# SwiGLU FFN on one core: gate and up of tokens 1024 to 2047 as seven block products instead of eight

## The chip, the cores and the metric

The kernel runs on one NeuronCore of a Trainium2 chip. A core has five engines with a queue each: TensorE (matmuls; PE in the profile), VectorE (DVE), ScalarE (ACT), GpSimd (POOL) and SyncE (SP, which here only issues DMAs). Matmuls write to PSUM, eight banks of 128 partitions by 512 fp32 numbers; VectorE and ScalarE read PSUM, and everything else lies in SBUF. The metric is the device time of the launch in microseconds.

## The reference

`x` has 2048 tokens of 512 numbers, `w_gate` and `w_up` are 512 by 1376, `w_down` is 1376 by 512, all in bf16:

```python
g = _silu(x @ w_gate)
u = x @ w_up
return (g * u) @ w_down
```

## The kernel before

Tokens are cut into four chunks c of 512 (`SC`), the 1376 hidden columns into ten tiles ft of 128 and a rest of 96, the 512 inputs into four blocks dk of 128. x lies transposed in `xT_sb` (block, token); the first 256 tokens are transposed on TensorE (the T groups), the others by transposing DMAs (`load_x`, one for tokens 256 to 511 and one per later chunk). SyncE issues all loads in one order (`loads_on_sync`): the first x, the weights in five slabs (gate, up), the last 32 up columns, x1, x2, x3, then `w_down`.

For each chunk and tile, a gate group and an up group of matmuls run on TensorE (`gu_step`, line 346): for each dk two half-wide matmuls of 64 weight columns each, 512 tokens, side by side in the array, into one PSUM bank. ScalarE writes silu of the gate bank to `sg_sb` (fp32, line 294), VectorE multiplies it with the up bank into `hT_sb` in bf16 (line 308). The rest of 96 columns is done by one X group per chunk (line 408) and one Y group per two chunks (line 419): their products go into `ht_sb`, in which each chunk has a strip of 32 partitions, and `hl_sb`.

Then comes the down stage. A product of an output tile of 128 tokens is summed over ten 128-row tiles of hidden columns and the rest. `strips` (line 455) cuts the 128 rows into four strips of 32 and runs four output tiles (a quad: one of each chunk) side by side, each in another strip of the array, in four turns; `whole_rows` (line 432) does the last quad with full 128-row matmuls. The finished bank is copied to `o_sb` by VectorE (line 312) or ScalarE and stored by a DMA.

The order on each engine is written out by hand as one list per engine: TensorE goes through chunk 0, 1, 2, 3 (tiles 0 to 9, then X), then Y, then down. A list of groups gives each group the next of the eight banks in turn, and a group waits until the readers of the group eight before it are done (`free`). Semaphores count finished groups (`s_P`) and finished operations of ScalarE and VectorE (`s_A`, `s_D`). GpSimd only makes one index pattern at the start (`iota`, line 278).

```python
for m in (0, HC):
    ins = pe.matmul(
        g["bank"][m:m + HC, n0:n1], lhsT=w_sb[:, dk, col + m:col + m + HC],
        rhs=xT_sb[:, dk, c * SC + n0:c * SC + n1], start=(dk == 0), stop=(dk == KD - 1),
```

Of the kernel before, what the change touches and what calls it, by code (L numbers as in the profile page):

```python
# [7 lines left out]
FP32 = mybir.dt.float32  # L8

N_WARM = 6  # L10
N_FILL = 1


def bass_standalone__swiglu_ffn__prompt_kernel(nc, x, w_gate, w_up, w_down, out):
# [3 lines left out]
    KD = D // P  # L18
    NFF = F // P
    NFT = NFF + 1  # L20
# [13 lines left out]
    NSG = 4  # L34
    NOS = 8
    assert D == 512 and S % SC == 0 and KD == 4 and F_LAST == 96 and NSC % 2 == 0
# [4 lines left out]

    UPH = F + 32
    WTOT = 2 * F
    XC0 = NFF * P
    YC0 = UPH + NFF * P

    with ExitStack() as es:
# [5 lines left out]
        w_sb = sb("w_sb", [P, KD, WTOT], BF16)  # L53
# [7 lines left out]
        sg_sb = [sb(f"sg_sb{i}", [P, SC], FP32) for i in range(NSG)]  # L61
        sgx_sb = [sb(f"sgx_sb{c}", [P, SC], FP32) for c in range(NSC)]
        sgy_sb = [sb(f"sgy_sb{c}", [P, SC], FP32) for c in range(NSC)]
        yu_sb = [sb(f"yu_sb{i}", [P, SC], FP32) for i in range(NSC // 2)]
        o_sb = [sb(f"o_sb{i}", [P, D], BF16) for i in range(NOS)]
        psum = ps("psum", [P, NB, 512], FP32)
        banks = [psum[:, i, :] for i in range(NB)]
        turn = [0, 2, 1, 3, 4, 5, 6, 7]

# [4 lines left out]
        s_I = sem("s_I")  # L74
        s_J = sem("s_J")
        s_P = sem("s_P")
        s_A = sem("s_A")
        s_D = sem("s_D")
        s_T = sem("s_T")
        s_dma = [sem(f"s_dma{i}") for i in range(4 * NOS)]  # L80
        rest = list(range(4 * NOS))

        def take(i):
            rest.remove(i)
            return s_dma[i]
# [3 lines left out]
        loads = {}  # L89

        def load_sem(name):
            loads[name] = take(homes[name] if name in homes else rest[0])
            return loads[name]
# [4 lines left out]


        def load_x(eng, name, t0, t1):  # L100
            eng.dma_start_transpose(
                xT_sb[:, :, t0:t1], xf[t0:t1, :]
            ).then_inc(load_sem(name), 16)

        def load_w(eng, name, src, base, f0, f1):
            eng.dma_start(
                w_sb[:, :, base + f0:base + f1],
                src[:, f0:f1].rearrange("(k p) f -> p k f", p=P),
            ).then_inc(load_sem(name), 16)

        slabs = [(0, 2), (2, 4), (4, 6), (6, 8), (8, NFT)]
        slab_of = {ft: a for a, b in slabs for ft in range(a, b)}

        def load_slab(eng, a, b):
            load_w(eng, f"wg{a}", w_gate, 0, a * P, min(b * P, F))
            load_w(eng, f"wu{a}", w_up, UPH, a * P, min(b * P, F - 32))

        def loads_on_sync(sp):
            sp.dma_start(
                xn_sb[:, :, :].rearrange("p j d -> p (j d)"), xf[0:HT, :].rearrange("(p j) d -> p (j d)", j=NXN)  # L120
            ).then_inc(load_sem("xn"), 16)
            load_slab(sp, *slabs[0])
            load_x(sp, "x0b", HT, SC)
            for a, b in slabs[1:]:
                load_slab(sp, a, b)
            load_w(sp, "wut", w_up, F - (F - 32), F - 32, F)
            for c in range(1, NSC):
                load_x(sp, f"x{c}", c * SC, (c + 1) * SC)
            sp.dma_start(
                wd_sb[:, 0:NFF, :], w_down[0:NFF * P, :].rearrange("(k p) d -> p k d", p=P)  # L130
            ).then_inc(load_sem("wd"), 16)
            for c in range(NSC):
                sp.dma_start(
                    wdt_sb[R * c:R * (c + 1), :, :], w_down[NFF * P:F, :].rearrange("(q p) d -> p q d", p=R)
                ).then_inc(load_sem(f"wdt{c}"), 16)
            sp.dma_start(wdl_sb[:, :], w_down[NFF * P:F, LASTA:D]).then_inc(load_sem("wdl"), 16)

        groups = []  # L140
        n_read = {"A": 0, "D": 0}
        act_ops, dve_ops = [], []

        def add_group(kind, **what):
            g = dict(kind=kind, at=len(groups), bank=banks[turn[(len(groups) - KD) % NB]], readers=[], **what)
            groups.append(g)
            return g

        def add_op(eng, g, **what):
            n_read[eng] += 1  # L150
            op = dict(g=g, at=n_read[eng], **what)
            (act_ops if eng == "A" else dve_ops).append(op)
            if g:
                g["readers"].append((eng, op["at"]))
            return op
# [7 lines left out]
        sg_reader = []  # L163
        n_sg = 0
        h_ready = {}

        def plan_tiles(c, fts):
            nonlocal n_sg
            gates = [add_group("G", c=c, ft=ft) for ft in fts]
            ups = [add_group("U", c=c, ft=ft) for ft in fts]  # L170
            for ft, gg, gu in zip(fts, gates, ups):
                b = n_sg % NSG
                free = sg_reader[n_sg - NSG] if n_sg >= NSG else 0
                a = add_op("A", gg, kind="silu", out=sg_sb[b][:, :], src=gg["bank"][:, :], free=free)
                d = add_op(
                    "D", gu, kind="mul", out=hT_sb[:, ft, c * SC:(c + 1) * SC], a=sg_sb[b][:, :],
                    b=gu["bank"][:, :], after=a["at"],
                )
                sg_reader.append(d["at"])
                h_ready[c] = d["at"]  # L180
                n_sg += 1
# [4 lines left out]
        LC = NSC - 1  # L186
        t_ready = {}

        def plan_x(c):
            g = add_group("X", c=c)  # L190
            y0, y1 = yblk(c)
            add_op("A", g, kind="silu", out=sgx_sb[c][96:128, :], src=g["bank"][64:96, :], free=0)
            a = add_op("A", g, kind="silu", out=sgy_sb[c][y0:y1, :], src=g["bank"][0:64, :], free=0)
            add_op(
                "D", g, kind="mul", out=ht_sb[R * c:R * (c + 1), 2, :],
                a=sgx_sb[c][96:128, :], b=g["bank"][96:128, :], after=a["at"] - 1,
            )
            if c == LC:
                add_op(
                    "D", g, kind="mul", out=hl_sb[2 * R:3 * R, :],  # L200
                    a=sgx_sb[c][96:128, SC - P:SC], b=g["bank"][96:128, SC - P:SC], after=a["at"] - 1,
                )

        def plan_y(pi):
            g = add_group("Y", pi=pi)
            a = add_op("A", g, kind="copy", out=yu_sb[pi][:, :], src=g["bank"][:, :], stored=(None, 0))
            for c in (2 * pi, 2 * pi + 1):
                y0, y1 = yblk(c)
                if c == LC:
                    add_op(  # L210
                        "D", None, kind="mul", out=hl_sb[0:2 * R, :],
                        a=sgy_sb[c][y0:y1, SC - P:SC], b=yu_sb[pi][y0:y1, SC - P:SC], after=a["at"],
                    )
                for q in range(2):
                    r0, r1 = y0 + R * q, y0 + R * (q + 1)
                    d = add_op(
                        "D", None, kind="mul", out=ht_sb[R * c:R * (c + 1), q, :],
# [97 lines left out]
        def on_tensor(pe):  # L315
# [111 lines left out]
            def whole_rows(g, start, stop):  # L427
                if start:
                    free(g)
# [115 lines left out]
```

## Time and profile before

| what | us |
|---|---|
| median of 3 runs | 120.28 (120.11 to 120.47) |
| span of the profiled execution, first to last instruction | 119.3 |
| TensorE busy | 116.5 (98%) |
| VectorE busy | 43.5 (36%) |
| ScalarE busy | 35.5 (30%) |
| GpSimd busy | 0.4 |
| matmuls of gate and up (line 346) | 71.0 summed |

The profile gives no time of the profiled execution beside its span; what lies around the span is seen as the difference to the runs' median. The page lists busy time per engine, the chain of work that ended last (followed back from the last instruction), and groups of instructions with their count, their summed busy time and the mean of one in ns. "Idle before" is how long the engine stood idle before the instructions of a group, and the arrow names what ended that. In the time line a row has start, length, engine, line, what is written and read, and how many instructions were merged into it; the length of a merged row runs from the first start to the last end. A matmul's own duration there includes its way through the array, so that successive matmuls overlap; their spacing is read from the chain, or from the instructions that wait for them.

### The profile page before, as it was taken

How to read it: one execution, taken by the hardware profiler on the slowest of the kernel's cores; microseconds unless marked ns; L12 is line 12 of the kernel's file. 1: busy time of each engine (PE TensorE's matmuls, PEld its weight loads, DVE VectorE, ACT ScalarE, POOL GpSimd, SP SyncE). 2: the span in 40 equal slices, each digit the busy share in tenths (PEclk: the TensorE clock that was granted, in tenths of full speed). 3: DMA queues.
4: the chain of work that ended last, by engine and by line, in shares of the span. 5: the costliest groups of instructions: out<-in, count | busy, mean ns of one | idle time of the engine just before them, and what ended most of it. 6: DMA issues, size and time to landing. Idle time of an engine off the chain costs nothing.

```text
span 119.3 us, 2971 instructions
## 1 busy us (share of the span) xinstructions
PE 116.5 (98%) x1333; PEld 65.9 (55%) x1334; DVE 43.5 (36%) x68; ACT 35.5 (30%) x61; POOL 0.4 (0%) x5
## 2 busy tenths in 40 slices
PE   7999999999999999999999999999999999999993
PEld 2796555555555555555555555554444444464452
DVE  0113534442534452444352444369800040224331
ACT  4225243264242365232454323470000030213001
POOL 1000000000000000000000000000000000000000
DMA  2999999990000000000000000000000023050612
GB/s 97 232 322 347 180 239 246 273 286 17 0 5 0 0 0 0 5 0 5 0 5 0 0 0 0 5 0 0 5 0 0 5 86 96 0 176 17 208 44 88
DMA packets 17564, 8.92 MB, mean 75 GB/s; under 512 B 8592, under 2 KB 17424, under 8 KB 17552
## 3 DMA queue, kind: packets, MB, share of 16 engines
q1 hardware_dynamic: 17408, 8.65, 28.5%
q8 instruction: 10, 0.16, 0.6%
q10 hardware_dynamic: 144, 0.10, 0.3%
q14 instruction: 2, 0.02, 0.1%
HBM read 4.81 MB, written 2.10 MB: 58 GB/s over the span
## 4 chain that ended last, share of the span: by engine, by line
PE 98%; DVE 0%; issue 0%
PE psum L346 59%; PE psum L455 24%; PE psum L432 7%; PE psum L408 3%; PE psum L360 2%; PE psum L419 1%; PE psum L375 0%; PE psum L383 0%; DVE o_sb L312 0%; PE psum L365 0%; PE psum L507 0%
## 5 line engine op out<-in xcount | busy, mean ns | idle before, releaser
L346 PE MATMUL psum<-xT_sb,w_sb 128*64 128x512 bf16 (+1 forms) x672 | 71.0, 374 | 0.0
L346 PEld LDWEIGHTS psum<-xT_sb,w_sb 128*64 128x64 bf16 x672 | 42.7, 112 | 27.4
L308 DVE TENSOR_TENSOR hT_sb<-sg_sb,psum 128x512 bf16<-128x512 f32 x40 | 27.5, 688 | 41.5 <-PE psum L346 36.6
L294 ACT ACTIVATE sg_sb<-psum 128x512 f32<-128x512 f32 x40 | 23.8, 596 | 41.6 <-PE psum L346 41.6
L455 PE MATMUL psum<-wd_sb,hT_sb 32*128 32x512 bf16 x480 | 26.9, 374 | 0.0
L455 PEld LDWEIGHTS psum<-wd_sb,hT_sb 32*128 32x128 bf16 x480 | 12.9, 93 | 13.1 <-issue 0.4
L312 DVE CAST o_sb<-psum 128x512 bf16<-128x512 f32 (+1 forms) x11 | 6.4, 604 | 25.1 <-PE psum L455 19.9
L294 ACT ACTIVATE o_sb<-psum 128x512 bf16<-128x512 f32 (+1 forms) x7 | 3.7, 580 | 33.0 <-PE psum L455 25.9
L432 PE MATMUL psum<-wd_sb,hT_sb 128*128 128x512 bf16 (+2 forms) x59 | 8.7, 307 | 0.2 <-issue 0.2
L432 PEld LDWEIGHTS psum<-wd_sb,hT_sb 128*128 128x128 bf16 x60 | 4.6, 98 | 4.6 <-issue 0.4
L308 DVE TENSOR_TENSOR ht_sb<-sgy_sb,yu_sb 32x512 bf16<-32x512 f32 x8 | 5.5, 683 | 0.4
L408 PE MATMUL psum<-xT_sb,w_sb 128*64 128x512 bf16 x32 | 4.2, 379 | 0.0
L308 DVE TENSOR_TENSOR ht_sb<-sgx_sb,psum 32x512 bf16<-32x512 f32 x4 | 2.8, 691 | 3.5 <-ACT sgx_sb L294 3.5
L294 ACT ACTIVATE sgx_sb<-psum 32x512 f32<-32x512 f32 x4 | 2.4, 588 | 4.5 <-PE psum L408 4.5
L360 PE MATMUL psum<-const-bfloat16-1.0 128*128 128x512 bf16 x6 | 2.7, 623 | 0.8 <-PEq L530 0.8
L455 PE MATMUL psum<-wdt_sb,ht_sb 32*128 32x512 bf16 (+1 forms) x48 | 3.3, 371 | 0.0
L408 PEld LDWEIGHTS psum<-xT_sb,w_sb 128*64 128x64 bf16 x32 | 2.0, 110 | 1.4
L294 ACT ACTIVATE sgy_sb<-psum 64x512 f32<-64x512 f32 x4 | 2.4, 591 | 0.1
L455 PEld LDWEIGHTS psum<-wdt_sb,ht_sb 32*128 32x128 bf16 x48 | 1.3, 93 | 1.3
L419 PE MATMUL psum<-xT_sb,w_sb 128*64 128x512 bf16 x16 | 1.9, 379 | 0.0
L360 PEld LDWEIGHTS psum<-const-bfloat16-1.0 128*128 128x128 bf16 x6 | 0.7, 133 | 1.9 <-issue 1.9
L283 ACT ACT_TABLE_LOAD x1 | 1.3, 1283 | 0.7 <-PEq L530 0.7
(21 smaller groups left out, 7.5 us busy)
## 6 DMA issues: line engine op xcount, KB each, us to landing
out_dram<-o_sb SPq DMA_DIRECT2D x15, 128.0 KB, 1.8
wd_sb<-in_w_down_dram SPq DMA_DIRECT2D x1, 1280.0 KB, 7.8
w_sb<-in_w_gate_dram SPq DMA_DIRECT2D x4, 256.0 KB, 4.0
w_sb<-in_w_up_dram SPq DMA_DIRECT2D x4, 256.0 KB, 4.2
wdt_sb<-in_w_down_dram SPq DMA_DIRECT2D x4, 96.0 KB, 8.1
w_sb<-in_w_gate_dram SPq DMA_DIRECT2D x1, 352.0 KB, 6.3
w_sb<-in_w_up_dram SPq DMA_DIRECT2D x1, 320.0 KB, 6.5
xn_sb<-in_x_dram SPq DMA_DIRECT2D x1, 256.0 KB, 2.8
```

Of the source, the lines that this page charges most:

```text
L283: act.activation(adummy[:, 0:4], zero_c, ACT.Silu)
L294: act.activation(op["out"], op["src"], fn).then_inc(s_A, 1)
L308: ins = dve.tensor_tensor(op["out"], op["a"], op["b"], ALU.mult)
L312: ins = dve.tensor_copy(op["out"], op["src"])
L346: ins = pe.matmul(g["bank"][m:m + HC, n0:n1], lhsT=w_sb[:, dk, col + m:col + m + HC], rhs=xT_sb[:, dk, c * SC + n0:c * SC + n1], start=(dk ...
L360: pe.matmul(banks[NB - 1][:, 0:width], lhsT=ones_w, rhs=ones_m[:, 0:width], start=True, stop=True)
L408: ins = pe.matmul(g["bank"][m:m + HC, :], lhsT=w_sb[:, dk, XC0 + m:XC0 + m + HC], rhs=xT_sb[:, dk, c * SC:(c + 1) * SC], start=(dk == 0), ...
L419: ins = pe.matmul(g["bank"][y0:y1, :], lhsT=w_sb[:, dk, YC0:YC0 + 64], rhs=xT_sb[:, dk, c * SC:(c + 1) * SC], start=(dk == 0), stop=(dk == ...
L432: ins = pe.matmul(g["bank"][:, 0:c1 - c0], lhsT=hT_sb[:, fk, t * P:(t + 1) * P], rhs=wd_sb[:, fk, c0:c1], start=(start and fk == 0), stop= ...
L455: ins = pe.matmul(g["bank"][:, 0:c1 - c0], lhsT=h(r, g["t"]), rhs=w[R * r:R * (r + 1), c0:c1], start=(start and n == 0), stop=final, tile_ ...
```

## The change

Chunks 0 and 1 and the rest columns are computed as before. For chunks 2 and 3 the ten hidden tiles are taken in five pairs, the units. Let A be the weights of a pair of tiles (f0, f1) and B the transposed x, each cut in two along the 512 inputs, and let C be the result, two tiles by two chunks. The plain way takes eight block products of 256 by 128 by 512, each of two matmuls, for gate and for up. The new way is the Winograd form of Strassen's method with seven:

- sums of weights S1 = A21 + A22, S2 = S1 - A11, S3 = A11 - A21, S4 = A12 - S2 (`w_sums`, on GpSimd, 128x256 each, for gate and up), and sums of x T1 = B12 - B11, T2 = B22 - T1, T3 = B22 - B12, T4 = B21 - T2 (`x_sums`, on VectorE, once, 128x1024 each), all kept in 4-byte fp32r; A22 and B22 are copied to fp32r beside them, since both operands of a matmul have one type;
- products P1 = A11 B11 and P2 = A12 B21 in bf16 (`two`), P3 = S4 B22, P4 = A22 T4, P5 = S1 T1, P6 = S2 T2, P7 = S3 T3 in fp32r (`four`), all with full 128-column weights;
- results C11 = P1 + P2, C12 = P1 + P6 + P5 + P3, C21 = P1 + P6 + P7 + P4, C22 = P1 + P6 + P7 + P5.

The products are summed in PSUM. A unit has six banks: X, Y and W, each for gate and up; X alternates between two pairs. P1 goes to X and is copied to Y (ScalarE for gate, VectorE for up). P6 is added to X, ScalarE copies X to SBUF (`keep(2)`), P7 is added, ScalarE copies again (`keep(3)`), P4 is added: C21. P2 is added to Y: C11. W gets P5; VectorE adds the kept X to it (C22), P3 is added to W, and VectorE adds the other kept X (C12). C11 and C21 go through silu and a VectorE product as before (`direct`); C12 and C22 go through VectorE sums in SBUF (`ts_sb`), silu, and a product on GpSimd (`sums`).

Every operation now goes into a `Plan`. TensorE and SyncE keep the order in which operations are added; those of ScalarE, VectorE and GpSimd are put in order when the kernel is built, by a list scheduler with fixed costs in ns: the operation that can start first comes next, and its priority breaks ties. Semaphore waits are derived from what each operation reads and writes. In the order that comes out, VectorE's five `x_sums` stand after the sixth product of chunk 0, with one product between each two; GpSimd does the sums of units 0 to 3 first, then unit 4's mixed with the first of its ten products. The X and Y groups of chunks 2 and 3 move into chunk 1, and the first eight pieces of the down stage are put between the last unit's P7 and P3. The loads and their order, the number of stores and the work of the down stage stay the same.

```diff
+PE_STEP, PE_STEP4, PE_LAG = 216, 231, 205
+A_BUSY, A_LAG = 485, 180
+D_BUSY, D_LAG = 610, 130
...
+            for n, op in enumerate(loose):
+                for e in op.engs:
+                    s = start(op, e)
+                    if s is not None and (best is None or (s, op.prio, n) < best[:3]):
+                        best = (s, op.prio, n, op, e)
...
-        sg_sb = [sb(f"sg_sb{i}", [P, SC], FP32) for i in range(NSG)]
...
+        sg_sb = [sb(f"sg_sb{i}", [P, SC], FP32) for i in range(6)]
+        ts_sb = [sb(f"ts_sb{i}", [P, SC], FP32) for i in range(4)]
+        r_sb = [sb(f"r_sb{i}", [P, SC], FP32) for i in range(6)]
...
+        ss_sb = sb("ss_sb", [P, NSLOT, 5, 2, KH, P], F32R)
+        tt_sb = sb("tt_sb", [P, 5, KH, SC], F32R)
...
+        def w_sums(u, eng, prio):
...
+                args = [
+                    ("S1", A21, A22, ALU.add, ()), ("S3", A11, A21, ALU.subtract, ()),
+                    ("S2", rd("S1"), A11, ALU.subtract, ["S1"]), ("S4", A12, rd("S2"), ALU.subtract, ["S2"]),
+                ]
+                for n, a, b, alu, of_ in args:
+                    tt_op(eng, at(n), a, b, alu, [wkey] + [key(o) for o in of_], [key(n)], prio, 670 if eng == "G" else 380)
+                plan.add(
+                    eng, lambda e, o=at("A22"), i=A22: e.tensor_copy(o, i), [wkey], [key("A22")], 330, G_LAG, prio
+                )
+
+        def x_sums(pi, eng, prio):
...
+            for n, a, b, alu, of_ in [
+                ("T1", B12, B11, ALU.subtract, ()), ("T3", B22, B12, ALU.subtract, ()),
+                ("T2", B22, rd("T1"), ALU.subtract, ["T1"]), ("T4", B21, rd("T2"), ALU.subtract, ["T2"]),
+            ]:
+                tt_op(eng, at(n), a, b, alu, xk + [("tt", o) for o in of_], [("tt", n)], prio, 1150)
+            plan.add(eng, lambda e: e.tensor_copy(at("B22"), B22), xk, [("tt", "B22")], 1100, D_LAG, prio)
+
+        class Unit:
...
+            def four(self, n, m, a, b, dst, start):
+                s, t = ss_sb[:, self.slot, W_SUM[a], m, :, :], tt_sb[:, X_SUM[b], :, :]
+
+                def emit(e):
+                    for k in range(KH):
+                        ins = e.matmul(
+                            bank(dst), lhsT=s[:, k, :], rhs=t[:, k, :], start=(start and k == 0),
+                            stop=(k == KH - 1), skip_group_check=True,
+                        )
+                    return ins
+                pe(emit, [("ss", self.slot, a, m), ("tt", b)], [("b", dst)], KH, PE_STEP4)
...
+            def p1(self):
+                for m in range(2):
+                    self.two(m, 0, self.X[m], True)
+                for m in range(2):
+                    copy_op("AD"[m], bank(self.Y[m]), bank(self.X[m]), [("b", self.X[m])], [("b", self.Y[m])], 0)
+
+            def keep(self, n):
+                for m in range(2):
+                    t, k = ring("r", r_sb)
+                    self.r[n, m] = t, k
+                    copy_op("A", t, bank(self.X[m]), [("b", self.X[m])], [k], 0)
+
+            def p6(self):
+                for m in range(2):
+                    self.four("P6", m, "S2", "T2", self.X[m], False)
+                self.keep(2)
...
+            def direct(self, b, ft, c):
+                sg, ksg = ring("sg", sg_sb)
+                silu_op(sg, bank(b[0]), [("b", b[0])], [ksg], 2)
+                tt_op("D", hview(ft, c), sg, bank(b[1]), ALU.mult, [ksg, ("b", b[1])], [("h", ft, c)], 2, D_BUSY)
+
+            def sums(self, n, ft, c):
+                parts = []
+                for m in range(2):
+                    (r, kr), (t, kt) = self.r[n, m], ring("ts", ts_sb)
+                    tt_op("D", t, r, bank(self.W[m]), ALU.add, [kr, ("b", self.W[m])], [kt], 1, D_BUSY)
+                    parts.append((t, kt))
+                (g, kg), (v, kv) = parts
+                sg, ksg = ring("sg", sg_sb)
+                silu_op(sg, g, [kg], [ksg], 3)
+                tt_op("G", hview(ft, c), sg, v, ALU.mult, [ksg, kv], [("h", ft, c)], 3, 1250)
...
-            strips(qa, body(1), True, False)
...
+        def down_start():
+            strips(qa, body(1)[:8], True, False)
...
+        for fts in [[2, 3]] + [[ft] for ft in range(4, NFF)]:
+            classic(0, fts)
+        plan_x(0, next_bank())
+        for ft in range(2):
+            classic(1, [ft])
+        plan_x(1, next_bank())
+        plan_y(0, next_bank())
+        for u in range(NSLOT):
+            w_sums(u, "G", 8)
+        x_sums(1, "D", 9)
+        for ft in range(2, 5):
+            classic(1, [ft])
+        plan_x(2, next_bank())
+        plan_x(3, next_bank())
+        plan_y(1, next_bank())
+        for ft in range(5, NFF - 1):
+            classic(1, [ft])
...
+        units[0].p1()
+        classic(1, [NFF - 1], [6, 7])
+        for u in range(NU):
+            unit = units[u]
+            unit.p6()
+            unit.p2()
+            unit.p5()
+            unit.p7()
...
+                units[u + 1].p1()
+            else:
+                down_start()
+                unit.p3()
+            unit.p4()
+            if u + 1 < NU:
+                unit.p3()
+        down()
```

852 lines of the change are left out of this document (504 added, 348 removed).

## The prediction

> **What bounds the kernel now.** I read the page's first part, then the chain of waits in order of time.
>
> ```profile
> span 119.3 us, 2971 instructions
> PE 116.5 (98%) x1333; PEld 65.9 (55%) x1334; DVE 43.5 (36%) x68; ACT 35.5 (30%) x61; POOL 0.4 (0%) x5
> ```
>
> ```profile
> 23.02 0.86 PE psum L408 x8
> 23.89 17.27 PE psum L346 x160
> ...
> 42.02 17.27 PE psum L346 x160
> ...
> 60.15 17.27 PE psum L346 x160
> ...
> 80.00 28.60 PE psum L455 x525
> 108.60 0.16 issue
> 108.76 8.34 PE psum L432 x49
> ```
>
> TensorE is the chain almost to the end, with one gap of 0.16 us. A chunk's gate and up take 17.27 us for 160 half-wide matmuls, 80 full ones: 216 ns per 512 columns. So only TensorE time, saved or lost, moves the end; VectorE and ScalarE count where a bank or an operand comes late. The sum is made against this span, 119.3 us; the median of the runs, 120.28, lies 0.98 above it, and I carry that over.
>
> **The change part by part.** *Removed:* for chunks 2 and 3, ten tiles of gate and up, 2 x 17.27 = 34.54 us.
>
> *Added on TensorE:* five units of 28 full matmuls: 8 in bf16 (p1, p2) and 20 in fp32r (p3 to p7). The bf16 ones go at 216 ns: 40 x 0.216 = 8.64 us. The trace has no 4-byte matmul; the nearest rows are the full 128x128 matmuls of the last output tiles.
>
> ```profile
> L432 PEld LDWEIGHTS psum<-wd_sb,hT_sb 128*128 128x128 bf16 x60 | 4.6, 98 | 4.6 <-issue 0.4
> ```
>
> ```profile
> 113.06 0.69 DVE L312 CAST o_sb<-psum 128x512 bf16<-128x512 f32 x1 [1.47 <-PE psum L432]
> ...
> 115.22 0.69 DVE L312 CAST o_sb<-psum 128x512 bf16<-128x512 f32 x1 [1.47 <-PE psum L432]
> ```
>
> The casts stand 2.16 us apart, ten matmuls each: 216 ns, with the 98 ns weight load hidden. Below that I exclude a gain: the 512 columns still pass. The upper end is a weight load put in series, 216 + 98 = 314. A load of twice the bytes, 196 ns, would still hide under 216, so I stay near the lower end and take the planner's own entry, 231 ns: its other entries agree with rows (216 here; 485, 610 and 711 against 0.50, 0.60 and 0.712 below). So 100 x 0.231 = 23.10, with 8.64 makes 31.74, and the saving is **2.80 us** (4.30 at 216, -5.50 at 314; nothing at 259).
>
> *Six switches of array layout* (half-width to full and back round p1, full to strips and back round p3 and p4, full to strips again). The one switch from strips to full shows 0.16 us of issue, that from half-width to strips at 80.00 none: 0 to 1.0 us in all, and I take **0.3**.
>
> *What stands beside TensorE in a unit.* Durations:
>
> ```profile
> L308 DVE TENSOR_TENSOR hT_sb<-sg_sb,psum 128x512 bf16<-128x512 f32 x40 | 27.5, 688 | 41.5 <-PE psum L346 36.6 <-ACT sg_sb L294 4.9
> ...
> L294 ACT ACTIVATE sg_sb<-psum 128x512 f32<-128x512 f32 x40 | 23.8, 596 | 41.6 <-PE psum L346 41.6
> ```
>
> ```profile
> 79.54 1.10 ACT L294 ACTIVATE yu_sb<-psum 128x512 f32<-128x512 f32 x2
> ...
> 80.17 4.25 DVE L308 TENSOR_TENSOR ht_sb<-sgy_sb,yu_sb 32x512 bf16<-32x512 f32 x6
> ```
>
> ```profile
> 108.63 1.29 DVE L312 CAST o_sb<-psum 128x512 bf16<-128x512 f32 x2 [3.68 <-PE psum L455]
> ```
>
> Back to back, an ACT starts every 0.50 (1.10 - 0.60), a VectorE op every 0.60 from PSUM (1.29 - 0.69) and 0.712 with two SBUF inputs ((4.25 - 0.69) / 5).
>
> ```profile
> 41.84 6.44 PE L346 MATMUL psum<-xT_sb,w_sb 128*64 128x512 bf16 x58
> 42.05 0.59 ACT L294 ACTIVATE sgx_sb<-psum 32x512 f32<-32x512 f32 x1 [1.13 <-PE psum L408]
> 42.66 0.59 ACT L294 ACTIVATE sgy_sb<-psum 64x512 f32<-64x512 f32 x1
> 42.74 0.69 DVE L308 TENSOR_TENSOR ht_sb<-sgx_sb,psum 32x512 bf16<-32x512 f32 x1 [0.86 <-ACT sgx_sb L294]
> ```
>
> TensorE to reader: 0.21 us after the next group's first matmul (41.84 to 42.05); ACT to VectorE 0.10. From p6's start a unit takes 6.35 us: p6 to 0.92, p2 1.79, p5 2.71, p7 3.64, the next p1 4.50, p4 5.42, p3 6.35. ACT does nine operations at 0.60, 5.4 us of it; VectorE seven at 0.69, 4.8. ACT in the planned order: keep(2) 0.67 to 1.9, silu Y to 2.5, last unit's silu to 3.1, keep(3) 3.4 to 4.6, copy X to Y to 5.2, silu to 5.8, silu X to 6.4. The tightest hand-backs: p7 wants keep(2) at 2.71 (0.8 spare), p4's second half wants keep(3) at 4.96 (0.4), p5's second half in the next unit wants its bank back from the second ts sum at 8.6 (sum over by 8.5 without any overlap of instructions, 0.1; with 0.60 spacing 0.6). So a unit stays bound by TensorE, at no cost by these rows; if reads of PSUM ran 0.2 us longer, the loop would lose some 0.3 each, 1.5 in all.
>
> *POOL* gets 50 sums and copies of 256 columns and 10 products of 512. Nearest row:
>
> ```profile
> L278 POOL IOTA diag<- 128x128 int32 x1 | 0.2, 236 | 0.4 <-POOLq L530 0.4
> ```
>
> For 256 columns 0.47, twice that for two inputs, 0.94. At the upper end a unit's sums take 8 x 0.94 + 2 x 0.47 = 8.5 us, four units 34 us from the first weights' arrival near 4.5: done by 38.5, while p6 first asks near 46. Unit 4's come after unit 0, asked for 25 us later. The last product (1.9 at the upper end) has about 3 us between its inputs and the strip that reads it, since `down` starts with pieces 0 to 7. Cost nothing; cover gone only at over three times these prices.
>
> *VectorE's x_sums* are the place where I expect a stall. Five operations of 1024 columns: from 0.293 at 128 columns (next fence) and 0.688 at 512 the slope is 1.03 ns a column, so 1.22 us each, 1.14 spaced. They need x3, the last transposed load, and VectorE's queue is in order: T1 stands after six products, the rest of them behind it.
>
> ```profile
> L308 DVE TENSOR_TENSOR hl_sb<-sgx_sb,psum 32x128 bf16<-32x128 f32 x1 | 0.3, 293 | 0.0
> ```
>
> ```profile
> L101 SPq DMA_TRANSPOSE xT_sb<-in_x_dram x2: 1712/2202/2691, 14.9 to 16.7; - x2
> ...
> DMA to landing us min/median/max: 4.6/4.7/4.8
> ```
>
> ```profile
> 17.88 0.69 DVE L308 TENSOR_TENSOR hT_sb<-sg_sb,psum 128x512 bf16<-128x512 f32 x1 [1.04 <-PE psum L346]
> ...
> 23.06 0.69 DVE L308 TENSOR_TENSOR hT_sb<-sg_sb,psum 128x512 bf16<-128x512 f32 x1 [1.04 <-PE psum L346]
> ```
>
> x3 is issued at 16.7 and lands near 21.4; the loads are not changed. The product that started at 17.88 (tile 6) now waits behind T1 and ends near 23.3. The product of 23.06 shows tile 9 over on TensorE at 22.85, so its bank is wanted after X(0), at 23.71: 0.4 spare. Each further pair (sum and product, 1.75) matches a tile's 1.73: spares 0.4, 0.4, 0.35. Then comes the fifth operation, the B22 copy (1.14), and only then X(0)'s product, over at 30.3; TensorE wants that bank for the up matmuls of chunk 1's tile 2 at 29.75. **0.55 us lost.** Afterwards VectorE catches up.
>
> *Down stage:* the same strips and whole-tile matmuls, reordered. `down_start` begins 3.64 us into unit 4, and its seventh piece, six times 0.218 (28.60 x 4 / 525) later at 4.95, reads unit 3's last product, whose silu is over at 3.2: with POOL's 0.94 to 1.9 it is there at 4.1 to 5.1. Nothing, at most 0.15. DMA issues: the same loads and stores, each queue in its old order; SP's and POOL's queues carry no new DMA.
>
> Sum: -2.80 + 0.55 + 0.30 = -1.95: span 117.35, **time 118.3 us**. Its own range is 117.0 to 119.4, from 216 to 235 ns per fp32r matmul and 0 to 1 us for either loss.
>
> **Rivals.**
> (a) *fp32r at 216 ns and x_sums and switches without loss*: 120.28 - 4.30 = 116.0. For it, the hidden load above; against it, the late x3.
>
> (b) *VectorE and POOL hinder each other in the x_sums.* POOL has sums to do until 30 or so, exactly while T1 to T4 run. If each T waits for the POOL operation under way, from half of the short one (0.24) to all of the long one (0.94), four of them add 0.9 to 3.8 on top of the 0.55, since the spare is used up already: 119.2 to 122.1; I take 119.8, nearer to the lower end, because the product between two T's (0.60) covers most of a POOL operation. Trace against or for: POOL is idle there, nothing shows it. The Trainium skill (SBUF — State Buffer, Who interferes with whom, and the section on two separate sides) says that the pair of ports that both share is an exclusive lock, taken for a whole instruction, and that a VectorE operation with two SBUF inputs wants it against a POOL operation that reads SBUF. By that rule the four sums, each with two SBUF inputs, would lose time and the PSUM products would not.
>
> (c) *The weight load of an fp32r matmul is not hidden:* slower than before. Place: every four(); price 314 - 231 = 83 ns x 100 = 8.3 us, so 126.6. It decides from 250 ns a matmul on, where 25.9 us of removed work, less 0.85 of losses, is used up. For it: the load handles twice the bytes; against it: 118 ns of each 216 stand free beside a 98 ns load.
>
> (d) *Four passes per fp32r matmul*, 0.864 us each: 120.28 + 86.4 - 25.9 + 0.85 = 181.6, the change not doing what it says. The Trainium skill (FP8 and Floating Point Precision, TensorE Precision Notes) gives four passes for true FP32 and beside it a reduced reading of 4-byte FP32, cut to about 22 bits; which of these fp32r is, and at what rate, no run here shows yet. That the rate of the reduced one is 216 or 231 ns is my reading.
>
> (e) *The unit loop is late by hand-overs*, 0.5 to 1 us in each of five units: 120.8 to 123.3 on top of the forecast's 118.3. For it: spares of 0.1 and 0.4; against it: ACT has 0.95 us of slack per unit and VectorE 1.5.
>
> **How the numbers follow.** Forecast 0.50; (a) 0.13; (b) 0.15; (c) 0.06; (d) 0.03; (e) 0.13. Range: the forecast with most of (a) and (b) and the lower part of (e), 116.2 to 121.6; it leaves out (c), (d), the upper half of (e) and little of (a), near 0.18. No change, within 0.3% (119.92 to 120.64, about what a measurement of this kernel can tell from none): a third of (b), 0.05. Faster: forecast, (a) and over half of (b), 0.71. Slower: the rest of (b) and (c), (d), (e), 0.24.
>
> **What would show it.** Right: the fp32r groups of a unit 0.92 us apart on the chain, units 6.35 us long; TensorE idle near 29.8 for half a microsecond, released by VectorE's product of X(0); T1 starting near 21.4; POOL's sums over before 40. Wrong: p6 or p7 at 0.64 us a pair or more (c) or over 1.7 (d); T2 to T4 starting later than the product before them ends (b); TensorE idle before p4, p5 or p6 in every unit (e). If x3 lands much earlier or later than 21.4, the stall moves one for one.

## The result and the profile after

The changed kernel takes 126.23 us (median of 4 runs, 125.57 to 126.91) against 120.19 us: a ratio of 1.0526, 95% interval 1.0470 to 1.0582. It is slower by 6 us, where 118.3 had been forecast. The profiled execution is one of 126.91 us, with a span of 125.6.

The first lines of the page of the changed kernel:

```profile
span 125.6 us, 2693 instructions
PE 116.4 (93%) x1150; PEld 66.2 (53%) x1154; DVE 61.9 (49%) x88; ACT 47.5 (38%) x86; POOL 42.0 (33%) x65
```

TensorE has fewer matmuls than before (1150 against 1333), and by the forecast it was to have 2.5 us less work; but its busy time is the same, and its share fell from 98% to 93%. So time is lost in two ways: it stands idle, and it works more slowly somewhere. The chain of waits shows where (start, length, what):

```profile
17.26 4.93 DMA xT_sb<-in_x_dram
22.49 5.86 issue
28.34 0.69 DVE hT_sb L318
29.03 0.14 issue
29.17 6.35 PE psum L392 x32
...
54.74 1.13 PE psum L540 x4
55.87 0.88 PE psum L552 x4
...
59.47 2.77 PE psum L540 x12
...
81.37 0.88 PE psum L552 x4
...
84.11 1.84 PE psum L680 x32
85.95 2.04 PE psum L540 x8
87.99 26.87 PE psum L680 x493
```

Line 392 is the half-wide gate and up, line 540 an fp32r product (`four`), line 552 a bf16 product (`two`), line 680 the strips of the down stage. Two things stand out. Between the landing of x3 (22.2) and 29.17 the chain holds no TensorE work: only 0.69 us of a VectorE product, and 5.86 us called "issue", in which no engine was waiting for anything that the profile knows. And the first 32 matmuls after it take 6.35 us; a tile of 16 takes 1.73 elsewhere, so they should have taken 3.45.

From 52 us on the chain is unbroken: the pieces of 0.07 and 0.16 us that it calls "issue" there, four in all, stand where the trace lacks the record of a matmul (it has 1154 weight loads and 1150 matmuls). Unit 0's P2 starts at 55.87 and unit 4's at 81.37: four units in 25.50 us, 6.38 each.

VectorE's time line over the gap names the instruction:

```profile
22.28 6.14 DVE L318 TENSOR_TENSOR tt_sb<-xT_sb 128x1024 fp32r<-128x1024 bf16 x1 [5.89 <-DMA xT_sb<-in_x_dram]
28.34 0.68 DVE L318 TENSOR_TENSOR hT_sb<-sg_sb,psum 128x512 bf16<-128x512 f32 x1
28.94 1.21 DVE L318 TENSOR_TENSOR tt_sb<-xT_sb 128x1024 fp32r<-128x1024 bf16 x1
...
34.14 0.68 DVE L524 CAST tt_sb<-xT_sb 128x1024 fp32r<-128x1024 bf16 x1
```

T1, the first of the x_sums, is recorded as running for 6.14 us; T3, the same operation on the same shape, takes 1.21. And on GpSimd, the first and the last of the forty sums of weights of units 0 to 3 (eight of the forty are the copies), with nothing else between them:

```profile
4.44 1.29 POOL L318 TENSOR_TENSOR ss_sb<-w_sb 128x256 fp32r<-128x256 bf16 x2 [3.38 <-DMA w_sb<-in_w_gate_dram]
...
26.66 0.68 POOL L318 TENSOR_TENSOR ss_sb<-w_sb,ss_sb 128x256 fp32r<-128x256 bf16 x1
```

GpSimd's row ends at 27.34, and T1 ends 1.1 us later, at 28.42: about its own length. T1 looks as if it had started only when GpSimd was done.

The table by stretches gives the other half. Its columns are length, busy time and count of PE, PEld, DVE, ACT and POOL, then the granted clock, and at the end the DMA's share and GB/s:

```profile
27.00:27.50 0.50, 0.00 (x0) 0.00 (x0) 0.50 (x1) 0.00 (x0) 0.34 (x1) 1.00 0.92 186
27.50:28.00 0.50, 0.00 (x0) 0.00 (x0) 0.50 (x1) 0.00 (x0) 0.00 (x0) 0.86 0.36 66
```

```profile
29.00:31.00 2.00, 1.83 (x10) 1.00 (x12) 2.00 (x4) 0.00 (x0) 0.00 (x0) 0.50 0.03 8
31.00:34.00 3.00, 3.00 (x18) 1.49 (x16) 3.00 (x4) 0.60 (x1) 0.00 (x0) 0.50 0.00 0
34.00:35.00 1.00, 1.00 (x10) 0.48 (x8) 0.97 (x3) 0.46 (x1) 0.00 (x0) 0.66 0.00 0
35.00:40.00 5.00, 5.00 (x50) 2.95 (x48) 4.18 (x7) 2.53 (x6) 0.00 (x0) 1.00 0.00 0
```

The clock fell from 1.00 to 0.50 near 27.9 (0.86 over the half microsecond from 27.5), some 4.5 us after TensorE's last matmul, and came back near 34.7, 5.5 us after it began again. The ledger against the forecast, span against span (125.6 and 117.35, 8.25 apart): TensorE idle for 5.81 us where 0.55 was forecast, 5.26; 6.35 instead of 3.45 for the first 32 matmuls, 2.9. Together 8.16 of the 8.25. That the two come so near the whole is in part chance: the changes of array layout and the units took 0.44 and 0.14 us more than forecast (see below), and chunk 0 was over some 0.5 us sooner than in the kernel before (X(0) starts at 22.33 in the time line, against 22.84).

### The profile page after: what moved, and what is told of

Same layout as the page of the kernel before. It is cut to its first block, busy times and chain, and to the rows that moved or that the text cites. A ratio compares the mean times of both kernels' runs of the same rounds, so it can differ in the third digit from the quotient of the medians.

```text
span 125.6 us, 2693 instructions
## 1 busy us (share of the span) xinstructions
PE 116.4 (93%) x1150; PEld 66.2 (53%) x1154; DVE 61.9 (49%) x88; ACT 47.5 (38%) x86; POOL 42.0 (33%) x65
## 4 chain that ended last, share of the span: by engine, by line
PE 75%; SPq 13%; issue 6%; DMA 4%; DVE 1%; DVEq 0%
PE psum L680 23%; PE psum L540 19%; PE psum L392 16%; PE psum L719 7%; PE psum L552 7%; SPq L257 7%; SPq L269 6%; DMA xT_sb<-in_x_dram 4%; PE psum L438 2%; PE psum L464 1%; DVE hT_sb L318 1%; SPq L274 0%; DVE o_sb L307 0%; PE psum L725 0%; DVE tt_sb L318 0%
## 5 line engine op out<-in xcount | busy, mean ns | idle before, releaser
L392 PE MATMUL psum<-xT_sb,w_sb 128*64 128x512 bf16 (+1 forms) x352 | 38.7, 379 | 6.1 <-DVE hT_sb L318 5.8
L392 PEld LDWEIGHTS psum<-xT_sb,w_sb 128*64 128x64 bf16 x352 | 21.4, 115 | 22.6 <-issue 9.3
L540 PE MATMUL psum<-tt_sb,ss_sb 128*128 128x512 f32 x100 | 26.8, 412 | 0.0
L318 POOL TENSOR_TENSOR ss_sb<-w_sb 128x256 fp32r<-128x256 bf16 x20 | 13.0, 675 | 33.3 <-PE psum L540 29.9
L540 PEld LDWEIGHTS psum<-tt_sb,ss_sb 128*128 128x128 f32 x100 | 18.6, 188 | 5.6 <-DVE ts_sb L318 0.4
L680 PEld LDWEIGHTS psum<-wd_sb,hT_sb 32*128 32x128 bf16 x480 | 12.8, 93 | 13.2 <-issue 0.4
L318 POOL TENSOR_TENSOR hT_sb<-sg_sb,ts_sb 128x512 bf16<-128x512 f32 x10 | 12.9, 1293 | 13.5 <-ACT sg_sb L313 11.8
L318 DVE TENSOR_TENSOR ts_sb<-r_sb,psum 128x512 f32<-128x512 f32 x20 | 12.8, 682 | 6.0 <-ACT r_sb L306 5.0
L306 ACT ACTIVATE r_sb<-psum 128x512 f32<-128x512 f32 x20 | 10.9, 594 | 8.5 <-PE psum L540 8.5
L318 DVE TENSOR_TENSOR tt_sb<-xT_sb 128x1024 fp32r<-128x1024 bf16 x2 | 7.3, 3674 | 5.9 <-DMA xT_sb<-in_x_dram 5.9
L552 PE MATMUL psum<-xT_sb,w_sb 128*128 128x512 bf16 x37 | 9.7, 381 | 0.3 <-issue 0.2
```

The source lines that it names most:

```text
L306: return e.activation(out, src, ACT.Copy)
L318: engs, lambda e: e.tensor_tensor(out, a, b, alu), reads, writes, busy,
L392: ins = e.matmul(psum[h:h + HC, b, n0:n1], lhsT=w_sb[:, dk, m, ft * P + h:ft * P + h + HC], rhs=xT_sb[:, dk, c * SC + n0:c * SC + n1], sta ...
L540: ins = e.matmul(bank(dst), lhsT=s[:, k, :], rhs=t[:, k, :], start=(start and k == 0), stop=(k == KH - 1), skip_group_check=True,)
L552: ins = e.matmul(bank(dst), lhsT=w_sb[:, k0 + k, m, f:f + P], rhs=xT_sb[:, k0 + k, c:c + SC], start=(start and k == 0), stop=(k == KH - 1) ...
L680: ins = e.matmul(psum[:, g["bank"], 0:c1 - c0], lhsT=h(r, g["t"]), rhs=w[R * r:R * (r + 1), c0:c1], start=(start and n == 0), stop=final, ...
```

## The experiments

Ten kernels, each changed from the kernel after unless it is said to build on another. Experiments 1, 4 and 10 have four times each, the others are a single execution with its trace: its time can show a hold of several microseconds, but no difference of a few tenths.

**1. The x_sums wait for GpSimd's row.** The same operations on the same engines; only their overlap is taken away.

```diff
         for u in range(NSLOT):
             w_sums(u, "G", 8)
-        x_sums(1, "D", 9)
+        x_sums(1, "D", 9, after=[op for op in plan.ops if op.engs == "G"][-1:])
```

> The five x_sums wait for the last of GpSimd's first 40 sums, so T1 starts near 27.3 with GpSimd idle and the loads over. Theory L (a VectorE operation with two SBUF inputs waits for GpSimd's whole row of back-to-back operations; the idle then halves TensorE's clock): T1 takes 1.2 us instead of 6.1, TensorE's idle of 5.8 us and the half-clock stretch (2.9 us lost) both go: 126.2 - 8.7 = 117.5, faster than the kernel before. Theory D (the loads of w_down slow T1 while they write SBUF, until about 27): the same time, since the loads are over too. Theory S (the first sum is slow by itself, whatever stands beside): T1 takes 6 us again, the time stays at 124 to 126.

118.71 us (118.3 to 118.95) against 120.41: a ratio of 0.9847, 0.9825 to 0.9869. That is 1.5% faster, small but clear of the noise. The time line of VectorE, and then the chain, show T1 at its plain length and no gap:

```profile
28.16 1.22 DVE L318 TENSOR_TENSOR tt_sb<-xT_sb 128x1024 fp32r<-128x1024 bf16 x1
```

```profile
23.12 0.86 PE psum L438 x8
23.99 3.45 PE psum L392 x32
...
46.66 1.25 PE psum L540 x4
...
77.98 2.04 PE psum L540 x8
```

The x_sums now also stand clear of the late x3, whose own price experiment 9 shows (0.84 us of waiting). So some 6.7 of the 7.5 us hang on the overlap of one VectorE operation with GpSimd's row; without it the change is faster than before, as forecast. The time is 1.2 us above the 117.5 that was expected here; between the two profiled executions 0.6 of this is chunk 0, which was over later (X(0) at 22.96 in the time line, against 22.33), and 0.1 a wait before the first P6 (46.66). What is still open is what holds T1, and when.

**2. Only unit 3's sums wait for T1.** T1 then runs with GpSimd idle but the weight loads still under way; T2 to T4 run beside a young row of GpSimd.

```diff
-        for u in range(NSLOT):
-            w_sums(u, "G", 8)
-        x_sums(1, "D", 9)
+        x_sums(1, "D", 9)
+        t1 = plan.ops[-5:-4]
+        for u in range(NSLOT):
+            w_sums(u, "G", 8, after=t1 if u == NSLOT - 1 else ())
```

> GpSimd's sums of unit 3 (10 of the 40) wait for T1. GpSimd is then idle when x3 lands near 22.3 and busy for 5.7 us as soon as T1 is over. Theory L: T1 takes 1.2 us, and now the second sum, T3, takes about 6 us, until GpSimd is done near 29.3; TensorE idles some 5 us, about one tile later than in the changed kernel; 124 to 127. Theory D (loads): T1 is slow as before, until about 27, and T3 takes 1.2. A fair turn-taking of the port: T1 1.2, T3 at most 1.9; idle under 1 us, 118 to 119.

121.11 us. VectorE, and the first pair of GpSimd's sums after T1:

```profile
22.16 1.23 DVE L318 TENSOR_TENSOR tt_sb<-xT_sb 128x1024 fp32r<-128x1024 bf16 x1 [5.41 <-DMA xT_sb<-in_x_dram]
...
23.90 1.38 DVE L318 TENSOR_TENSOR tt_sb<-xT_sb 128x1024 fp32r<-128x1024 bf16 x1
...
25.80 1.72 DVE L318 TENSOR_TENSOR tt_sb<-xT_sb,tt_sb 128x1024 fp32r<-128x1024 bf16 x1
...
28.04 1.45 DVE L318 TENSOR_TENSOR tt_sb<-xT_sb,tt_sb 128x1024 fp32r<-128x1024 bf16 x1
```

```profile
23.53 2.28 POOL L318 TENSOR_TENSOR ss_sb<-w_sb 128x256 fp32r<-128x256 bf16 x2 [1.93 <-DVE tt_sb L318]
```

T1 beside the loads takes 1.23, so the DMAs do not slow it. But the sums beside GpSimd were not held for the rest of the row, as the theory had it: they lost 0.16 to 0.50 each. GpSimd lost as well: a pair of its sums that takes 1.30 took 2.28. Here the two engines took turns, and it is this case that rival (b) of the prediction had priced.

**3. The copy of B22 first.** It has one SBUF input, not two.

```diff
+            plan.add(eng, lambda e: e.tensor_copy(at("B22"), B22), xk, [("tt", "B22")], 1100, D_LAG, prio)
             for n, a, b, alu, of_ in [
...
-            plan.add(eng, lambda e: e.tensor_copy(at("B22"), B22), xk, [("tt", "B22")], 1100, D_LAG, prio)
```

> The copy of B22 (one SBUF input, 0.68 us in the changed kernel) goes first of the five, T1 fourth from the end. Theory L in its narrow form (only two SBUF inputs want the port): the copy takes 0.7 us at 22.3 and one product follows it at once; T1 is then held until GpSimd's end near 27.2; TensorE idles 3.5 to 4.5 us instead of 5.8. In its wide form (the fast one-input copy wants the port too): the copy takes about 5 us, until 27.2, and the idle is about as long as in the changed kernel, 5 to 6. Theory D: the copy is slow as well, until about 27.

126.5 us. VectorE:

```profile
22.46 5.57 DVE L519 CAST tt_sb<-xT_sb 128x1024 fp32r<-128x1024 bf16 x1 [5.72 <-DMA xT_sb<-in_x_dram]
...
28.55 1.21 DVE L318 TENSOR_TENSOR tt_sb<-xT_sb 128x1024 fp32r<-128x1024 bf16 x1
```

The copy, 0.68 us by itself, is held until 28.03, some 0.55 us after GpSimd's row ended (its last sum started at 26.78 and took 0.70); T1, which comes after the end of the row, takes 1.21. So an operation with one SBUF input can be held too. The Trainium skill (SBUF — State Buffer, Who interferes with whom) says that copies and casts can enter a two-port mode and then want the pair of ports shared with GpSimd as well; this row agrees with that. The products of a PSUM bank with `sg_sb`, which have one SBUF input and are no copies, ran at 0.68 to 0.69 us beside the row throughout.

**4. TensorE kept busy through the gap.** 26 needless matmuls before chunk 1, to part the two halves of the loss.

```diff
+        def fill(e):
+            for i in range(N_IDLE):
+                ins = e.matmul(bank(1), lhsT=ones_w, rhs=ones_m, start=True, stop=True)
+            return ins
+
+        pe(fill, (), [("b", 1)], 0)
         for ft in range(2):
             classic(1, [ft])
```

> As the changed kernel, with 26 needless matmuls (5.6 us) on TensorE in the place where it idles, ahead of chunk 1's first tile. If the half clock comes from the idle, it goes: TensorE starts chunk 1 at the same 29.2 but at full clock, 126.2 - 2.9 = 123.3. If the half clock has another cause (power of the sums, a fixed time), the time stays at 126 and the rows near 29 to 34 show 0.5 again.

124.82 us (124.65 to 124.84) against 120.41: a ratio of 1.0363, 1.0347 to 1.0378. TensorE:

```profile
23.65 5.63 PE L771 MATMUL psum<-const-bfloat16-1.0 128*128 128x512 bf16 x25 [0.16 <-issue]
29.29 3.64 PE L393 MATMUL psum<-xT_sb,w_sb 128*64 128x512 bf16 x32
...
35.81 0.41 PE L393 MATMUL psum<-xT_sb,w_sb 128*64 128x512 bf16 x2 [0.29 <-DVE ht_sb L319]
```

(One of the 26 has no record.) The granted clock stays at 1.0, and the 32 matmuls take 3.64 in the time line instead of 6.35. The hold of T1 is there as before (6.16 us). The time falls by 1.4 us (2.1 between the two spans), not by the 2.9: TensorE at full clock now catches up with VectorE, which is still behind with its x_sums, and waits for it a little later (the row at 35.81 is one of these waits). Some 0.8 of the 2.9 would thus have been lost to VectorE's lateness in any case; the half clock had covered it.

**5. A probe early in the row.** On top of experiment 1: a needless VectorE sum of two weight blocks, 128x256, behind the product of tile 3.

```diff
+        half = lambda k: w_sb[:, k:k + KH, 0, 0:P]
+        tt_op(
+            "D", ts_sb[0][:, 0:KH * P].rearrange("p (k f) -> p k f", k=KH), half(0), half(KH), ALU.add,
+            [f"wg{slab_of[0]}"], [("ts", 0)], 0, 380, after=[plan.writer["h", 3, 0]],
+        )
         plan_x(0, next_bank())
```

> As e1 (x_sums after GpSimd's 40 sums), plus one needless VectorE sum of two SBUF blocks of 128x256 (about 0.42 us alone) right behind the product of chunk 0's tile 3, near 12.7 us, in the middle of GpSimd's long row (4.4 to 27.3). Theory L (a VectorE operation that wants the port gets it only when the row is over): it takes some 14 us, until 27, all products behind it wait, TensorE idles from about 16 us on for 11 us or more and falls to half clock; 130 to 135. Turn-taking behind a product, as in e3: it takes at most 1.1 us and the time is that of e1, 118 to 119. A limit of some operations that stand in GpSimd's queue (about nine went by in the changed kernel): it takes about 5 us, and the time is 121 to 124.

128.75 us, a little under the 130 to 135 expected of a hold to the end of the row. VectorE and TensorE:

```profile
12.93 14.59 DVE L318 TENSOR_TENSOR ts_sb<-w_sb 128x256 f32<-128x256 bf16 x1
```

```profile
28.26 4.63 PE L392 MATMUL psum<-xT_sb,w_sb 128*64 128x512 bf16 x24 [8.39 <-DVE hT_sb L318]
```

The probe, a quarter of T1's size and on other data, is held for 14.59 us: to 27.52, 0.28 us after GpSimd's last sum (26.56 and 0.68 long). The hold ends with the row here too, and it needs neither x nor its loads nor an operation of T1's size.

**6. The row broken before T1.** The sums of units 2 and 3 wait for the product of tile 5, which stops GpSimd from 15.95 to 16.50. T1 comes 6.45 us after the restart.

```diff
         for u in range(NSLOT):
-            w_sums(u, "G", 8)
+            w_sums(u, "G", 8, after=[plan.writer["h", 5, 0]] if u > 1 else ())
```

> As the changed kernel, but GpSimd's sums of units 2 and 3 wait for the product of tile 5, so its row is interrupted for about 0.5 us near 16 and goes on from 16.5 to 28, with nine or so operations since its new start when T1 comes at 22.3. If what keeps T1 out is the length of GpSimd's unbroken row (its cores drifting apart), T1 now takes turns, at most 2 us, and the time is near e3's 121. If T1 is kept out by any row in which GpSimd's next operations stand ready, T1 takes until 28, 6 to 7 us, and the time is 126 to 127.

122.32 us. GpSimd after the pause, then VectorE:

```profile
16.50 1.29 POOL L318 TENSOR_TENSOR ss_sb<-w_sb 128x256 fp32r<-128x256 bf16 x2 [0.55 <-DVE hT_sb L318]
...
22.21 1.29 POOL L318 TENSOR_TENSOR ss_sb<-w_sb 128x256 fp32r<-128x256 bf16 x2
```

```profile
22.95 1.64 DVE L318 TENSOR_TENSOR tt_sb<-xT_sb 128x1024 fp32r<-128x1024 bf16 x1 [6.53 <-DMA xT_sb<-in_x_dram]
...
27.06 1.72 DVE L318 TENSOR_TENSOR tt_sb<-xT_sb,tt_sb 128x1024 fp32r<-128x1024 bf16 x1
```

A pause of half a microsecond, six microseconds earlier, turned a hold of 6.14 us into 1.64. T1 met the row at the same place in both runs: the second sum of a pair was under way, the 32nd of the forty, and eight were left. So neither the sum under way nor the number still to come decides. Two explanations were left: the hold needs a row that has run unbroken for long, or it is special to the first row, which starts on a DMA's semaphore and not on VectorE's.

**7. The probe earlier.** Experiment 5 with the probe behind tile 1's product, 5 us into the first row.

```diff
-            [f"wg{slab_of[0]}"], [("ts", 0)], 0, 380, after=[plan.writer["h", 3, 0]],
+            [f"wg{slab_of[0]}"], [("ts", 0)], 0, 380, after=[plan.writer["h", 1, 0]],
```

> Adds one needless VectorE sum (two SBUF inputs, 128x256) behind the product of tile 1 to the kernel in which the x_sums wait for POOL; the same probe behind the product of tile 3 was held from 12.93 to 27.5, to the end of POOL's row. It becomes ready here near 9.7 us, some 5 us and eight operations after POOL's row began at 4.44. Theory LENGTH (a row that has run unbroken for over some 6 to 8 us no longer lets VectorE in, a younger one does): the probe takes at most 1.1 us, TensorE loses nothing, 118.5 to 119.0 us. Theory FIRST (it is POOL's first row that holds, whatever its age; the rows that took turns were all started or restarted by a wait on VectorE): it is held from about 9.7 to 27, some 17 us, and the time is 130 us or more.

**8. The row broken early.** As experiment 6, but the sums of units 1 to 3 wait for tile 3's product: GpSimd stops from about 10.2 to 12.67 and then runs unbroken to 29.8.

```diff
-            w_sums(u, "G", 8, after=[plan.writer["h", 5, 0]] if u > 1 else ())
+            w_sums(u, "G", 8, after=[plan.writer["h", 3, 0]] if u > 0 else ())
```

> The sums of units 1, 2 and 3 wait for the product of tile 3 (near 13 us), so that POOL's row is broken from about 10 to 13 and then runs unbroken to about 30; x_sums as in the changed kernel. T1 becomes ready at 22.3, some 9 us and sixteen operations after the restart (6.4 us and ten operations after it, in the run with the later break, T1 took 1.64 us). Theory LENGTH: T1 is held to the end of the row near 30, 7 to 8 us, TensorE idle some 7 us, 127 to 129 us. Theory FIRST: they take turns, T1 to T4 at 1.4 to 1.8 us each, 121.5 to 122.5 us.

118.65 us for experiment 7 and 128.59 us for experiment 8. VectorE in experiment 7, then VectorE and GpSimd in experiment 8:

```profile
9.49 1.00 DVE L318 TENSOR_TENSOR ts_sb<-w_sb 128x256 f32<-128x256 bf16 x1
```

```profile
22.02 8.88 DVE L318 TENSOR_TENSOR tt_sb<-xT_sb 128x1024 fp32r<-128x1024 bf16 x1 [5.97 <-DMA xT_sb<-in_x_dram]
```

```profile
12.67 1.29 POOL L318 TENSOR_TENSOR ss_sb<-w_sb 128x256 fp32r<-128x256 bf16 x2 [2.41 <-DVE hT_sb L318]
...
29.16 0.66 POOL L318 TENSOR_TENSOR ss_sb<-w_sb,ss_sb 128x256 fp32r<-128x256 bf16 x1
```

Both came out as the theory of length had it, and against the other. In GpSimd's first row a probe 5 us after its start takes 1.00 us; in a row restarted by VectorE's own product T1 is held until 30.90, 1.1 us after the row's end. Put together, by the time from the row's last start to the VectorE operation:

| run | row unbroken for, us | operation | it took, us |
|---|---|---|---|
| 7, earlier probe | 5.0 | 128x256 sum | 1.00 |
| 6, broken before T1 | 6.45 | T1 | 1.64 |
| 5, probe | 8.55 | 128x256 sum | 14.59 |
| 8, broken early | 9.35 | T1 | 8.88 |
| after | 17.84 | T1 | 6.14 |
| 3, copy first | 17.88 | cast | 5.57 |

Each row is one execution; experiment 4 repeats the fifth (17.82 us, T1 6.16). Every operation in the upper two rows took turns, every one in the lower four was held to the end of the row. The border lies between 6.5 and 8.5 us of these sums; whether it is a time or a number of instructions (the twelfth and the fifteenth sum were under way), and why it exists at all, these runs do not tell.

**9. GpSimd's sums after the x_sums.** It takes the overlap away from the other side, and leaves only the late x3.

```diff
-        for u in range(NSLOT):
-            w_sums(u, "G", 8)
         x_sums(1, "D", 9)
+        xs = plan.ops[-5:]
+        for u in range(NSLOT):
+            w_sums(u, "G", 8, after=xs)
```

> All of GpSimd's sums wait for the x_sums, so T1 to T4 and the copy run at x3's landing with GpSimd idle: T1 1.2 us at 22.3, each of the four 1.2. TensorE then loses what the late x3 alone costs: 0.55 us at the bank of X(0), by the prediction. Afterwards GpSimd's row runs from about 28.5 to 52 beside the eight products with two SBUF inputs (sgy, yu). Theory L: the first of these is held until the row is over and TensorE idles some 15 us or more; 135 to 145. Turn-taking: each of the eight is up to 0.7 us longer, TensorE idles 0.5 to 2 us in all; 118.5 to 121.

121.96 us. T1 to T4 take 1.22 to 1.23 each, from 22.30 on. TensorE waits for VectorE twice:

```profile
24.27 3.64 PE L392 MATMUL psum<-xT_sb,w_sb 128*64 128x512 bf16 x32 [0.55 <-DVE hT_sb L318]
...
30.80 4.51 PE L392 MATMUL psum<-xT_sb,w_sb 128*64 128x512 bf16 x40 [0.29 <-DVE ht_sb L318]
```

This is the stall that the prediction had put at 0.55 us: 0.84 in all. The second of the two waits, for the bank of X(0), is the one it described; the first fits x3's landing at 22.2 instead of 21.4, 0.8 later where 0.4 were spare. The rest of the loss comes later: GpSimd starts at 30.01 and becomes the bound of the first units. The chain has it on the way from 57.9 to 64.0:

```profile
60.21 1.31 POOL ss_sb L318 x3
...
62.73 1.25 POOL hT_sb L318
```

**10. Sums kept in bf16.** Experiment 1 with `ss_sb` and `tt_sb` in bf16, so that all matmuls are bf16 ones and the sums are rounded.

```diff
-        ss_sb = sb("ss_sb", [P, NSLOT, 5, 2, KH, P], F32R)
-        tt_sb = sb("tt_sb", [P, 5, KH, SC], F32R)
+        ss_sb = sb("ss_sb", [P, NSLOT, 5, 2, KH, P], BF16)
+        tt_sb = sb("tt_sb", [P, 5, KH, SC], BF16)
```

> As e1, with the sums of weights and of x kept in bf16 instead of fp32r (they are rounded to bf16; the rest is the same, in the same order). The 100 matmuls of four() should go at 216 ns instead of 231: 1.5 us less than e1, 117.2, if TensorE's rate is all that fp32r costs. If the units are bound by hand-overs and not by TensorE, the time stays that of e1, 118.7. The x_sums themselves become faster (two-byte operands), at no gain.

116.14 us (115.93 to 116.86) against 120.42: a ratio of 0.9642, 0.9607 to 0.9676, the fastest of all. The chain, and the weight loads here and in the kernel after:

```profile
47.50 0.86 PE psum L552 x4
48.37 1.73 PE psum L540 x8
...
53.55 0.86 PE psum L552 x4
```

```profile
L540 PEld LDWEIGHTS psum<-tt_sb,ss_sb 128*128 128x128 bf16 x100 | 9.6, 98 | 12.2 <-DVE ts_sb L318 0.6 <-issue 0.4
```

```profile
L540 PEld LDWEIGHTS psum<-tt_sb,ss_sb 128*128 128x128 f32 x100 | 18.6, 188 | 5.6 <-DVE ts_sb L318 0.4 <-issue 0.4
```

A unit takes 6.05 us (47.50 to 53.55) instead of 6.38, some 1.7 us less over five units, and x_sums take 0.68 to 0.69 each instead of 1.22. Against experiment 1 the medians lie 2.6 apart, the spans 2.1 (115.5 against 117.6); the rest of these 2.1 lies at the first and last fp32r matmuls (0.97 and 1.83 us where experiment 1 has 1.25 and 2.04) and at the start.

## Why the prediction was wrong

*The step that failed* is VectorE's x_sums: "0.55 us lost", with each of the five at 1.22 us or less, the length of an operation that nothing hinders. That held for all of them but the first, which took 6.14. The step before it, that POOL's sums "cost nothing" because unit 0's are asked for only near 46, looked at when their results are due and not at what GpSimd's running does to the engine beside it. That was put off to rival (b).

*Rival (b)* named the right place and the right pair of engines, and the side: slower. Its price was wrong. It let each T wait for one GpSimd operation under way, 0.24 to 0.94 us; experiments 2 and 6 show that this happens (0.2 to 0.5 us each), and give 121.1 and 122.3 us, inside rival (b)'s 119.2 to 122.1 or just above. But in a row that had run unbroken for 17.8 us the first T waited for the operation under way and all eight that were left, about 5 us, and the three after it, with GpSimd idle, for none. So the sign that the prediction gave for (b), T2 to T4 starting late, did not show, though (b)'s two engines were at work. The Trainium skill (SBUF — State Buffer, Who interferes with whom) gives the shared pair to whoever issues first, for the whole instruction. As far as that goes the young rows agree (0.2 to 0.5 us lost by each T); the old rows do not: there VectorE got no turn between GpSimd's instructions, up to the end of the row.

*The second loss was in no term and in no rival:* the half clock after an idle TensorE, 2.9 us here and 1.4 of it gained back by filling the gap (experiment 4). A stall of 0.55 us would not have set it off: in experiment 6 TensorE was idle for 1.94 us, and the granted clock stayed at 1.0.

*The price of an fp32r matmul* was right, though taken over from the planner's entry and not worked out: 12 in 2.76 to 2.77 us on the chain are 230 to 231 ns each, and the unit takes 6.38 us where 6.35 was forecast. The weight load of 188 ns (the prediction had 196 as an estimate) stays hidden. Rivals (c) and (d) fall with it; that (c)'s 126.6 lies beside the measured time is chance. So does (e): from 52 us on the chain has no wait in the units.

*Rival (a)* falls as stated, since it wanted 216 ns of fp32r. That rate is what the bf16 sums of experiment 10 bring, at 116.1 us.

*The switches of layout* were under-sized, and the row they were read from was misread. The 0.16 us of "issue" at 108.60 is no switch but a matmul without a record (60 weight loads of line 432 on the page, 59 matmuls), and so is the 0.16 ahead of P1: in experiment 10, whose trace lacks none, the group that starts there has no gap in front. What shows is that the first group behind a change of layout takes longer than the same matmuls elsewhere: P1 0.97 instead of 0.86, chunk 1's tile 9 behind it 1.85 instead of 1.73, the first P6 1.13 instead of 0.92, the first 32 matmuls of the strips 1.84 instead of 1.74, the last eight fp32r matmuls 2.04 instead of 1.84 or 1.86. Together that is 0.74 against 0.3 forecast, and inside the 0 to 1.0. No run takes a switch away, so the cause is read from the place alone.

*The sum without the hold.* Experiment 1 gains 1.70 us; the forecast without its stall for x3 was 2.50. Of the 0.80 between them, 0.44 are the switches, 0.14 the units (five times 0.03), 0.12 a wait of the first P6 for VectorE's copy of P1, which came late behind T4 (1.25 instead of 1.13 on the chain), and 0.10 lie at the start: X(0) begins at 23.12 instead of 23.02.

*GpSimd's prices* were bounded rightly: a sum of 256 columns 0.67, a copy 0.40, a product 1.29, the forty sums over at 27.3, where the upper end gave 38.5. *The copy of B22* takes 0.68 us where 1.22 (1.14 spaced) was forecast, which makes VectorE's row shorter. *x3* was issued at 17.26 and landed 4.93 later, at 22.2; the prediction had taken 16.7 and 4.7 from the kernel before. These two errors work against each other: that its 0.55 us for the stall comes near the 0.84 of experiment 9 is in part luck. *The down stage* takes 28.71 us in its two pieces (1.84 and 26.87) against 28.60; the difference is counted with the switches.

## What to carry to other kernels

Before a spare engine is filled with a long row of work, ask what that work shares with the engine beside it: here forty small GpSimd sums, none of them urgent, cost some 7 us by holding one VectorE operation for 5. A price for contention "per instruction" is a lower end only; the upper end is the rest of the row. A break in the row brings it down to turns (experiment 6: 122.3 us), an order in which the sensitive operations come after the row avoids it (experiment 1: 118.7 us). A stall of TensorE of several microseconds is to be priced together with the half clock that follows it.

## What the runs showed of the hardware

- A VectorE sum of two SBUF inputs, or a cast from SBUF to SBUF, was held up to 14.59 us when GpSimd had run its sums back to back for 8.55 us or longer, always until GpSimd's row ended; VectorE's products of a PSUM bank were not (0.68 to 0.69 us). At 6.45 us or less the two took turns, and both lost: T's of 1.22 took up to 1.72 us, and pairs of GpSimd sums of 1.30 up to 2.28.
- A turn seems to start the count anew: in experiment 6 T3, T2 and T4 still took turns 8.6, 10.6 and 12.8 us after GpSimd's restart (1.43 to 1.72 us each), and in experiment 9 VectorE's products with two SBUF inputs 10 us after GpSimd's start at 30.01; but in both VectorE had taken a turn every few microseconds. This was seen, not tested.
- A held operation is shown as busy, not as waiting. The chain calls its time "issue"; only its length beside that of its neighbours (6.14 and 1.21) gives it away.
- The TensorE clock fell to 0.50 between 2.3 us (experiment 8, after 23.0) and 5.4 us (experiment 5, after 19.9) into an idle stretch, with 3.8 us in experiment 3 and 4.5 us in the kernel after; it came back 3.8 to 5.5 us after work began again. An idle stretch of 1.94 us (experiment 6) left it at 1.0. The Trainium skill (TensorE: Matmul & The Clock Gate, What's actually happening) gives at least one window of about 3.4 us, idle or busy, for either; the returns and most of the falls agree, the fall after 2.3 us came sooner.
